# First two blocks of a fused chunk-attention and FFN kernel: only the first third of the FFN columns in halves of 128 tokens

## The chip, the cores and the metric

The kernel runs on one core of one Trainium2 chip. The metric is the device time of one execution in microseconds (us); smaller is better. Eight runs of the kernel before stand behind its median. The profile is of one further execution, and its own times are used wherever a sum is made.

## The reference

Attention over chunks, followed by a gated feed-forward network (FFN). The inputs are float32, with batch 4, 8 heads, 768 tokens and a head dimension of 64; the FFN has 3072 tokens, a model width of 512 and 1536 FFN columns.

```python
k_min, k_max = k_chunks.min(3), k_chunks.max(3)        # chunks of 32 tokens
ub = sum(maximum(q * k_min, q * k_max))                # upper bound by query and chunk
top_chunks = argsort(where(causal, ub, -1e9))[..., -6:]
scores = where(sel & causal_by_token, q @ k.T / sqrt(D), -1e9)
x = (softmax(scores) @ v)                              # heads side by side: 3072 x 512
xn = x / sqrt(mean(x * x) + 1e-6) * rms_g
g = xn @ w_gate
out = (g * sigmoid(g) * (xn @ w_val)) @ w_out
```

## The kernel before

The work is cut into 12 blocks of 256 tokens, in the order of `ORDER` (line 398): the first block of each batch element, then later ones. A block belongs to one batch element `b` and a third `m` of its tokens. For each block, and for each of two groups of four heads, `job` (line 626) does the attention. DVE transposes K and Q (line 642), the copies `kb` and `qb` in bf16 are made on ACT or POOL (lines 649, 650), DVE reduces K to the minimum and maximum of each chunk (line 657), and DVE or POOL writes them into block-diagonal matrices BD (line 669). `pick` (line 531) multiplies these with Q on TensorE (line 562, the upper bounds), finds the six best chunks on DVE and turns the result into masks. TensorE makes scores and adds the masks (lines 720, 731), ACT takes the exponential into `pt` (line 770), POOL cuts the triangle off (line 740), TensorE multiplies with the values (line 796), and DVE divides by the row sum into `xnat` (lines 811, 815).

`norm` (line 822) follows. ACT squares and sums `xnat` (line 831), POOL makes the reciprocal root (lines 837, 839), DVE or ACT scales to `xs` (lines 847, 849), TensorE transposes (line 859), and DVE or ACT multiplies with `rms_g` into `xsT` (lines 872, 868).

`ffn` (line 879) then goes over the FFN columns. There are 12 tiles of 128 columns; the three thirds of the gate, value and output weights (`wg`, `wv`, `wo`) are loaded by nine transfers on POOL's queue (lines 516 and 521). For each step, TensorE makes one PSUM bank of gate products and one of value products (line 897), with 512 columns each: two column tiles for the 256 tokens of a block, or four for 128 tokens. ACT takes the tanh (`th`, line 904), DVE makes `tg` from it (line 908), and the product with the values, `hh`, is made in one of two ways: DVE reads the values from PSUM (line 912, the steps in `DIRECT`, line 407), or ACT copies them to `vs` (line 916) and POOL multiplies (line 919). TensorE multiplies `hh` with `wo` (line 929), and ACT or DVE takes the result to `osb` (lines 943, 945), which SP stores (line 950).

Blocks 0 and 1 are in `SPLIT` (line 404): `HALVES` (line 409) cuts them into two halves of 128 tokens, and both `norm` and `ffn` are called for each half. So a half goes through all three thirds of the columns by itself, in three steps of four column tiles. Each half takes one of the four `xsT` buffers.

Nothing of the order is left to the hardware or to a compiler. `plan.op` records each operation with its engine, an expected occupation and latency, and a priority; `Plan.run` (line 160) walks through a modelled time and gives each engine, at each point, the operation of the lowest priority number that could start. What comes out is a fixed order for each engine, and each engine works through its own from front to back. The priorities come from due times: `due_attn(i) = PACE * i - LEAD` and `due_ffn(i) = PACE * i` (lines 412 to 416), with offsets by step. Operations recorded with `flex` may go to one of two engines, and the walk chooses. `PATIENT` (line 120) lets an engine look a little ahead for an urgent operation. Where TensorE would be idle in the modelled time before 60 us, the walk puts in matmuls of constants (line 995), called filler here; they are executed.

SP issues the loads of K, Q and V of the blocks in order, and stores between them. `HELD` (line 475) makes a load wait for a weight transfer: for block 2 the first K load waits for the first gate third and the first V load for the first value third, and for block 3 both wait for the first third of `wo`. SP issues in order, so everything behind such a load waits too. There are two buffers for raw K, three for raw Q, two for raw V, four PSUM banks F (gate, value, output, value products and transposes) and two double banks S (scores and upper bounds).

The softmax here doesn't subtract the row's maximum and nothing guards it: scores larger than these inputs give would overflow.

## Time and profile before

| | |
|---|---|
| median of 8 runs | 305.92 us (305.17 to 306.32) |
| the profiled execution | 305.85 us |
| its span, first to last instruction | 304.1 us, granted TensorE clock 1.000 |
| gate and value matmuls (line 897) | 192 + 192 of 128 columns, 480 + 480 of 256 |
| output matmuls (line 929) | 288 of 512 columns |
| filler (line 995) | 86 of 128 columns, 36 of 512 in the program, 29 of these in the records |
| nine weight transfers (POOL's queue) | issued from 10.8 to 21.3 us |
| `hh` on POOL (line 919), on DVE (line 912) | 51 of 1.164 us, 21 of 0.687 us |

A row of the page's groups gives the line, engine, operation, what is written and read, shapes, count, busy time, mean duration, and the idle time before with what ended it. A row of a timeline gives the start, the duration, the engine and line, and in brackets the idle time before and its releaser. A row of windows gives a stretch and then, for each engine, the time in which it was busy. Matmuls overlap, so the start of one group to the start of the next is the better measure of its cost than the duration given. A few matmul records are missing from the trace.

### The profile page before, as it was taken

Reading aid. Unit: us, or ns where it says so; the run is one execution under the profiler, and the core shown is the slowest. Engines: PE = TensorE matmul, PEld = TensorE weight load, DVE = VectorE, ACT = ScalarE, POOL = GpSimd, SP = SyncE. Lnnn points to the kernel's source line nnn. Section 1 sums busy time; section 2 is a strip of 40 time slices with the busy share of each in tenths; the row PEclk is TensorE's granted clock in tenths of the full one; section 3 lists DMA queues with packets and bytes.
Section 4 is the critical chain, followed back from the end, with each engine's and each line's share of the span. In section 5 each row is a group of like instructions: output and inputs, shape, how many; then the busy total and the mean of one; then the engine's idle time right before and its main releaser. Section 6 shows DMA issues by size and latency. Waiting matters only on the chain.

```text
span 304.1 us, 11660 instructions
## 1 busy us (share of the span) xinstructions
PE 289.5 (95%) x4830; PEld 223.4 (73%) x4858; DVE 218.7 (72%) x565; ACT 217.4 (71%) x382; POOL 147.2 (48%) x267
## 2 busy tenths in 40 slices
PE   8777999999999999999999999999999999999994
PEld 8445897767958876885887787688588688588671
DVE  6997797886799999999999697286457254356250
ACT  3574975779987996997797856698767588476240
POOL 4694568758572784687456413235213143123130
PEclk9999999999999999999999999999999999999999
DMA  7999995775766556565850200100010010010101
GB/s 195 221 197 263 196 205 119 162 200 121 192 152 160 126 120 160 129 147 120 195 128 0 72 2 4 69 5 3 2 71 2 2 71 3 34 39 1 69 2 69
DMA packets 74837, 30.65 MB, mean 101 GB/s; under 512 B 65568, under 2 KB 70176, under 8 KB 74784
## 3 DMA queue, kind: packets, MB, share of 16 engines
q1 hardware_dynamic: 69184, 24.66, 33.4%
q0 software_dynamic: 4752, 4.72, 9.3%
q8 instruction: 38, 0.62, 0.8%
q10 hardware_dynamic: 848, 0.53, 0.6%
q14 instruction: 15, 0.12, 0.2%
HBM read 28.31 MB, written 6.29 MB: 114 GB/s over the span
## 4 chain that ended last, share of the span: by engine, by line
PE 76%; DVE 5%; ACT 2%; issue 1%
PE F L897 34%; PE F L929 20%; PE S L720 7%; PE F L796 6%; PE S L562 5%; PE S L731 2%; PE F L859 1%; DVE kx L657 1%; DVE tg L908 1%; ACT pt L770 1%; DVE xnat L815 1%; ACT junk L831 0%; DVE qT L642 0%; ACT xs L849 0%; DVE m L597 0%
## 5 line engine op out<-in xcount | busy, mean ns | idle before, releaser
L919 POOL TENSOR_TENSOR hh<-tg,vs 128x512 bf16<-128x512 bf16 x51 | 59.3, 1164 | 83.0 <-ACT vs L916 62.3
L770 ACT ACTIVATE pt<-S 128x1024 bf16<-128x1024 f32 (+3 forms) x104 | 86.2, 860 | 18.3 <-PE S L731 17.6
L897 PE MATMUL F<-xsT,wg 128*128 128x256 bf16 (+1 forms) x672 | 74.9, 257 | 2.3 <-DMA wg<-in_moe_w_gate_dram 1.6
L897 PE MATMUL F<-xsT,wv 128*128 128x256 bf16 (+1 forms) x672 | 74.9, 257 | 2.1 <-DMA wv<-in_moe_w_val_dram 1.3
L908 DVE SCALAR_TENSOR_TENSOR tg<-th,F 128x512 bf16<-128x512 bf16 x72 | 48.8, 680 | 36.7 <-ACT th L904 36.0
L929 PE MATMUL F<-wo,hh 128*128 128x512 bf16 x267 | 64.4, 379 | 1.7 <-issue 1.0
L897 PEld LDWEIGHTS <-wg 128*128 128x128 bf16 x672 | 56.6, 98 | 10.3 <-DMA wg<-in_moe_w_gate_dram 2.1
L897 PEld LDWEIGHTS <-wv 128*128 128x128 bf16 x672 | 56.8, 98 | 9.4 <-DMA wv<-in_moe_w_val_dram 1.5
L904 ACT ACTIVATE th<-F 128x512 bf16<-128x512 f32 x72 | 43.3, 602 | 17.1 <-PE F L897 15.7
L929 PEld LDWEIGHTS <-hh 128*128 128x128 bf16 x288 | 26.5, 98 | 28.5
L740 POOL TENSOR_SCALAR_AFFINE_SELECT pt<-pt 128x512 bf16<-128x512 bf16 x48 | 30.5, 645 | 18.1 <-ACT pt L770 17.4
L916 ACT ACTIVATE vs<-F 128x512 bf16<-128x512 f32 x51 | 30.7, 601 | 6.3 <-PE F L897 5.4
L720 PE MATMUL S<-qb,kb 32*128 32x256 bf16 (+1 forms) x800 | 32.6, 253 | 1.4 <-ACT qb L649 1.2
L657 DVE TENSOR_REDUCE kx<-kT 128x16 f32<-128x512 f32 x48 | 30.3, 663 | 0.0
L796 PE MATMUL F<-VX,pt 128*128 128x65 bf16 x672 | 26.7, 194 | 0.9 <-ACT vs L916 0.4
L796 PEld LDWEIGHTS <-pt 128*128 128x128 bf16 x672 | 24.2, 98 | 3.7 <-issue 1.1
L831 ACT ACTIVATE junk<-xnat 128x512 bf16<-128x512 bf16 x24 | 15.1, 627 | 14.2 <-DVE xnat L815 12.4
L720 PEld LDWEIGHTS <-kb 32*128 32x128 bf16 x800 | 13.6, 92 | 14.5 <-issue 13.7
L945 DVE TENSOR_SCALAR osb<-F 128x512 f32<-128x512 f32 x14 | 9.5, 687 | 17.6 <-PE F L929 17.6
L815 DVE TENSOR_TENSOR xnat<-F,rden 128x256 bf16<-128x256 f32 x48 | 19.8, 421 | 1.1
L731 PE MATMUL S<-mtd,chunkrow 32*128 32x128 bf16 (+2 forms) x384 | 20.3, 203 | 0.0
L731 PE MATMUL S<-mto,chunkrow 32*128 32x128 bf16 (+2 forms) x384 | 19.8, 202 | 0.0
(61 smaller groups left out, 357.0 us busy)
## 6 DMA issues: line engine op xcount, KB each, us to landing
vraw<-in_v_dram SPq DMA_DIRECT2D x24, 256.0 KB, 4.1
out_dram<-osb SPq DMA_DIRECT2D x24, 256.0 KB, 2.2
kraw<-in_k_dram SPq DMA_DIRECT2D x72, 64.0 KB, 3.0
qraw<-in_q_dram SPq DMA_DIRECT2D x72, 64.0 KB, 2.3
wg<-in_moe_w_gate_dram POOLq DMA_DIRECT2D x3, 512.0 KB, 14.0
wv<-in_moe_w_val_dram POOLq DMA_DIRECT2D x3, 512.0 KB, 17.0
wo<-in_moe_w_out_dram POOLq DMA_DIRECT2D x3, 512.0 KB, 24.6
kraw<-in_k_dram SPq DMA_DIRECT2D x10, 128.0 KB, 4.8
```

The costliest lines, as they stand in the source:

```text
L657: plan.op(f"ext{n}{J}", "DVE", 0.585, 0.67, lambda n=n, op=op: VE.tensor_reduce(out=at(kx)[:, n], in_=at(kT).rearrange("p h (c t) -> p h c ...
L720: TE.matmul(s[a // 2][:, a % 2, c0:c0 + q1 - q0], kbt[r, t, ks], qbt[r, t, q0:q1], start=(t == 0), stop=(t == 1 and not mask), skip_group_ ...
L731: TE.matmul(o, chunkrow[r, BLK * kg + P * e:BLK * kg + P * (e + 1)], mv, start=False, stop=(d == 1), skip_group_check=True)
L740: GE.affine_select(out=d, in_=d, compare_op=ALU.is_ge, fill=0.0, base=0, pattern=[[0, 4], [1, P]], channel_multiplier=-1)
L770: lambda pt=pt, hs=hs, c0=c0, c1=c1, x=sc[hp]: SE.activation(out=at(pt)[:, hs, c0:c1], in_=at(x)[:, :, c0:c1], func=ACT.Exp, scale=SCALE), ...
L796: TE.matmul(o[:, a, :], p_[:, a, off:off + P], vt[:, e, a, :], start=(kb_ == 0 and a == 0), stop=(kb_ == nkb - 1 and a == 3), skip_group_c ...
L897: TE.matmul(at(p_)[:, n * W:(n + 1) * W], w[:, g, ht * P:(ht + 1) * P], at(xT)[:, g, 0:W], start=(g == 0), stop=(g == NP - 1), skip_group_ ...
L904: plan.op(f"tanh{U}.{hp}", "ACT", 0.48, 0.6, lambda th=th, gp=gp: SE.activation(out=at(th), in_=at(gp), func=ACT.Tanh, scale=0.5), pri - 0 ...
L908: VE.scalar_tensor_tensor(out=at(tg), in0=at(th), scalar=1.0, in1=at(gp), op0=ALU.add, op1=ALU.mult), pri - 40, reads=[th, gp], writes=[tg ...
L916: plan.op(f"vcopy{U}.{hp}", "ACT", 0.48, 0.6, lambda vs=vs, vp=vp: SE.activation(out=at(vs), in_=at(vp), func=ACT.Copy), pri + 0.1, reads= ...
L919: plan.op(f"hh{U}.{hp}", "POOL", 1.11, 1.16, lambda tg=tg, vs=vs, hh=hh: GE.tensor_tensor(out=at(hh), in0=at(tg), in1=at(vs), op=ALU.mult) ...
L929: TE.matmul(at(op)[:], at(("hh", *U, ht // K))[:, o:o + P], wo[:, ht, :], start=(ht == 0), stop=(ht == NHT - 1))
```

## The change

For blocks 0 and 1, `norm` still goes by halves, but both halves write into one `xsT` buffer of 256 tokens, each into its own columns. `ffn` is called once for a block. It makes a list of pieces: for a block in `SPLIT`, the first third of the columns (four column tiles) for the first 128 tokens, the same for the second 128 tokens, and then the remaining eight tiles for all 256 tokens, two tiles at a time. The other blocks have six pieces of two tiles, as before. The output product picks its rows of `hh` from either kind of piece; its last step now has two column tiles in all blocks.

Beside this some settings change. Block 2's K and V loads both wait for the second gate third, and block 3's V load for the second `wo` third. `DIRECT` holds blocks 8 to 11 in place of 5 to 11, so nine `hh` products go from DVE to ACT and POOL. `PACE` and `LEAD` are 22.5 and 70 in place of 23.5 and 73, `PATIENT` is empty, and the priorities of tanh, of the direct `hh`, of the output product, of the output copy and of the first halves' `norm` differ. In the built program the gate and value matmuls are 64 + 64 of 128 columns and 544 + 544 of 256, and there are 38 wide fillers.

```diff
 
 
     SHARES = ("scale", "relu", "bd0", "bd1", "dk", "mk")
-    PATIENT = {"DVE": 0.3}
+    PATIENT = {}
     RESERVED = ("hh",)
     HOP = {"PE": 0.055, "ACT": 0.04, "DVE": 0.04, "POOL": 0.075, "SP": 0.06}
 
...
     ORDER = [(0, 0), (1, 0), (2, 0), (3, 0), (0, 1), (1, 1), (0, 2), (2, 1), (1, 2),
              (3, 1), (2, 2), (3, 2)]
     assert sorted(ORDER) == [(b, m) for b in range(B) for m in range(NBLK)]
-    PACE, LEAD = 23.5, 73
+    PACE, LEAD = 22.5, 70
     MARGIN = 2.0
     FIRST = 8
     SPLIT = {0, 1}
     APART = {0, 1}
     PACKED = {0, 1, 2}
-    DIRECT = {(i, hp) for i in range(len(ORDER)) for hp in range(KH) if i >= 5 and hp % 2}
+    DIRECT = {(i, hp) for i in range(len(ORDER)) for hp in range(KH) if i >= 8 and hp % 2}
 
     def HALVES(i):
         return ((0,), (1,)) if i in SPLIT else ((0, 1),)
...
     ones = [("ones", i) for i in range(len(store["VX"]))]
 
 
-    HELD = {2: (("wg", 0), ("wv", 0)), 3: (("wo", 0), ("wo", 0))}
+    HELD = {2: (("wg", 1), ("wg", 1)), 3: (("wo", 0), ("wo", 1))}
 
     def load_qk(i, nm, src):
         b, m = ORDER[i]
...
         blk = b * NBLK + m
         n = len(toks)
         U = (i, toks)
-        xT, tp = ("xsT", *U), ("tp", *U)
+        xT, tp = ("xsT", i), ("tp", *U)
+        cols = slice(toks[0] * P, (toks[-1] + 1) * P)
         for s in toks:
             xn, tt = ("xnat", b, m, s), 2 * blk + s
             plan.op(f"square{i}{s}", "ACT", 0.61, 0.82, lambda xn=xn, tt=tt: SE.activation(
...
 
         def rows():
             for g in range(NP):
-                SE.activation(out=at(xT)[:, g, 0:n * P], in_=tview()[:, g], func=ACT.Copy,
+                SE.activation(out=at(xT)[:, g, cols], in_=tview()[:, g], func=ACT.Copy,
                               scale=rmsg[:, g:g + 1])
 
         flex(f"xsT{U}", {
             "DVE": (0.07 + 0.53 * n, 0.15 + 0.53 * n, lambda: VE.tensor_tensor(
-                out=at(xT)[:, :, 0:n * P], in0=tview(),
+                out=at(xT)[:, :, cols], in0=tview(),
                 in1=rmsg[:].unsqueeze(2).to_broadcast([P, NP, n * P]), op=ALU.mult)),
-            "ACT": (0.6 + 0.43 * n, 0.72 + 0.43 * n, rows)}, base, reads=[tp, "rmsg"], writes=[xT],
-            takes=[(xT, "xsT")])
-
-
-    def ffn(i, toks):
+            "ACT": (0.6 + 0.43 * n, 0.72 + 0.43 * n, rows)}, base, reads=[tp, "rmsg"] + (
+                [xT] if toks[0] else []), writes=[xT + (s,) for s in toks],
+            takes=[] if toks[0] else [(xT, "xsT")])
+
+
+    def ffn(i):
         b, m = ORDER[i]
-        U = (i, toks)
-        W = P * len(toks)
-        K = 512 // W
-        KH = NHT // K
-        base = due_ffn(i) + toks[0]
-        xT = ("xsT", *U)
-        for hp in range(KH):
-            third = 3 * hp // KH
+        xT = ("xsT", i)
+        whole = (0, 1)
+        cut = NHT // 3 if i in SPLIT else 0
+        pieces = [((s,), h) for s in whole for h in range(0, cut, 4)] + [
+            (whole, h) for h in range(cut, NHT, 2)]
+        for toks, h0 in pieces:
+            W = P * len(toks)
+            K = 512 // W
+            U = (i, toks)
+            hp = h0
+            base = due_ffn(i) + toks[0]
+            third = 3 * h0 // NHT
+            x0 = P * toks[0]
             gp, vp = ("gp", *U, hp), ("vp", *U, hp)
             th, vs, tg, hh = ("th", *U, hp), ("vs", *U, hp), ("tg", *U, hp), ("hh", *U, hp)
-            pri = base + hp * 6 // KH
+            pri = base + h0 // 2
             for nm, p_, w in (("wg", gp, wg), ("wv", vp, wv)):
-                def gate(p_=p_, w=w, hp=hp):
+                def gate(p_=p_, w=w, h0=h0, K=K, W=W, x0=x0):
                     for n in range(K):
-                        ht = K * hp + n
+                        ht = h0 + n
                         for g in range(NP):
                             TE.matmul(at(p_)[:, n * W:(n + 1) * W],
-                                      w[:, g, ht * P:(ht + 1) * P], at(xT)[:, g, 0:W],
+                                      w[:, g, ht * P:(ht + 1) * P], at(xT)[:, g, x0:x0 + W],
                                       start=(g == 0), stop=(g == NP - 1), skip_group_check=True)
 
                 o = plan.op(f"{nm}{U}.{hp}", "PE", 0.873, 1.035, gate, pri,
-                            reads=[xT, (nm, third)], writes=[p_], takes=[(p_, "F")])
+                            reads=[xT, (nm, third)] + [xT + (s,) for s in toks], writes=[p_], takes=[(p_, "F")])
                 o.mode = "full"
             plan.op(f"tanh{U}.{hp}", "ACT", 0.48, 0.6, lambda th=th, gp=gp: SE.activation(
-                out=at(th), in_=at(gp), func=ACT.Tanh, scale=0.5), pri - 0, reads=[gp], writes=[th],
+                out=at(th), in_=at(gp), func=ACT.Tanh, scale=0.5), pri - 20, reads=[gp], writes=[th],
                 takes=[(th, "th")])
             plan.op(f"tg{U}.{hp}", "DVE", 0.6, 0.69, lambda th=th, gp=gp, tg=tg:
                     VE.scalar_tensor_tensor(
                         out=at(tg), in0=at(th), scalar=1.0, in1=at(gp), op0=ALU.add,
                         op1=ALU.mult), pri - 40, reads=[th, gp], writes=[tg], takes=[(tg, "tg")])
-            if (i, hp) in DIRECT:
+            if (i, h0 // 2) in DIRECT:
                 plan.op(f"hh{U}.{hp}", "DVE", 0.6, 0.69, lambda tg=tg, vp=vp, hh=hh: VE.tensor_tensor(
-                    out=at(hh), in0=at(tg), in1=at(vp), op=ALU.mult), pri - 40, reads=[tg, vp],
+                    out=at(hh), in0=at(tg), in1=at(vp), op=ALU.mult), pri - 30, reads=[tg, vp],
                     writes=[hh], takes=[(hh, "hh")])
                 continue
             plan.op(f"vcopy{U}.{hp}", "ACT", 0.48, 0.6, lambda vs=vs, vp=vp: SE.activation(
...
             plan.op(f"hh{U}.{hp}", "POOL", 1.11, 1.16, lambda tg=tg, vs=vs, hh=hh: GE.tensor_tensor(
                 out=at(hh), in0=at(tg), in1=at(vs), op=ALU.mult), pri - 40, reads=[tg, vs],
                 writes=[hh], takes=[(hh, "hh")])
-        for k_, s in enumerate(toks):
+        for s in whole:
             op, ob = ("op", i, s), ("osb", i, s)
-            last = NHT - K
-
-            def project(h0, h1, k_=k_, op=op):
+            last = NHT - 2
+
+            def part(ht, s=s):
+                if ht < cut:
+                    return ("hh", i, (s,), ht // 4 * 4), ht % 4 * P
+                return ("hh", i, whole, ht // 2 * 2), ht % 2 * BLK + s * P
+
+            def project(h0, h1, s=s, op=op, part=part):
                 for ht in range(h0, h1):
-                    o = (ht % K) * W + k_ * P
-                    TE.matmul(at(op)[:], at(("hh", *U, ht // K))[:, o:o + P], wo[:, ht, :],
+                    key, o = part(ht)
+                    TE.matmul(at(op)[:], at(key)[:, o:o + P], wo[:, ht, :],
                               start=(ht == 0), stop=(ht == NHT - 1))
 
-            pri = base + 8 + s
+            base = due_ffn(i)
+            hhs = sorted({part(ht)[0] for ht in range(last)}, key=str)
+            pri = base + 6 + s
             o = plan.op(f"project{i}.{s}", "PE", 0.216 * last, 0.216 * last + 0.17,
                         lambda project=project: project(0, last), pri,
-                        reads=[("hh", *U, x) for x in range(KH - 1)] + [("wo", x) for x in range(3)],
+                        reads=hhs + [("wo", x) for x in range(3)],
                         writes=[op], takes=[(op, "F")])
             o.mode = "full"
-            o = plan.op(f"project{i}.{s}+", "PE", 0.216 * K, 0.216 * K + 0.17,
+            o = plan.op(f"project{i}.{s}+", "PE", 0.216 * 2, 0.216 * 2 + 0.17,
                         lambda project=project: project(last, NHT), pri - 20,
-                        reads=[("hh", *U, KH - 1), op], writes=[op])
+                        reads=[part(NHT - 1)[0], op], writes=[op])
             o.mode = "full"
             flex(f"out{i}.{s}", {
                 "ACT": (0.48, 0.6, lambda op=op, ob=ob: SE.activation(
                     out=at(ob), in_=at(op), func=ACT.Copy, scale=0.5)),
                 "DVE": (0.6, 0.69, lambda op=op, ob=ob: VE.tensor_scalar(
                     out=at(ob), in0=at(op), scalar1=0.5, scalar2=None, op0=ALU.mult))},
-                pri - 0, reads=[op], writes=[ob], takes=[(ob, "osb")])
+                pri - 20, reads=[op], writes=[ob], takes=[(ob, "osb")])
             r0 = b * S + BLK * m + P * s
             o = plan.op(f"store{i}.{s}", "SP", 0.46, 0.46, lambda ob=ob, r0=r0: SY.dma_start(
                 out=out[r0:r0 + P, :], in_=at(ob)), pri, reads=[ob])
...
             for j in jobs:
                 next(j, None)
         for toks in HALVES(i):
-            norm(i, toks, due_attn(i) + (7 if toks[-1] else -12))
+            norm(i, toks, due_attn(i) + (7 if toks[-1] else -3))
         if i == 0:
             for n in range(3):
                 load_w(n, -290 if n == 0 else -36 + n)
...
                 if o.dma and o.eng == "POOL":
                     o.after.append(first_dk[0])
     for i in range(len(ORDER)):
-        for toks in HALVES(i):
-            ffn(i, toks)
+        ffn(i)
 
     def keep_busy(n, slot, wide):
         for _ in range(n):
```

## Prediction

> **What bounds the kernel now.** I read the busy table and the slices of the page first. TensorE (PE) leads, and its slices say when it is not full:
>
> ```profile
> PE 289.5 (95%) x4830; PEld 223.4 (73%) x4858; DVE 218.7 (72%) x565; ACT 217.4 (71%) x382; POOL 147.2 (48%) x267
> PE   8777999999999999999999999999999999999994
> DMA  7999995775766556565850200100010010010101
> ```
>
> Only the first four slices (7.6 us each), about 30 us, and the last lack 9s. Even those 7s flatter it: line 995 is filler (matmuls of a constant that keep the array busy), so I read the windows of that line, where PE is busy 6.55 us of the first 8 us, 4.29, 2.28, 1.20 and 0.38 us of the next 8 us stretches, then nothing. Useful work is thin until about 37 us and dense after. The windows of all engines, then PE's own waits between 60 and 200 us:
>
> ```profile
> 32.00:40.00 8.00, 7.83 (x163) 7.21 (x162) 6.54 (x15) 7.36 (x17) 5.75 (x8) 1.00 1.21 196
> 40.00:48.00 8.00, 7.37 (x144) 7.02 (x142) 7.57 (x13) 5.53 (x11) 5.59 (x14) 1.00 1.02 180
> 144.00:168.00 24.00, 23.79 (x445) 19.17 (x447) 22.66 (x59) 19.19 (x34) 13.16 (x25) 1.00 0.47 109
> ...
> PE F L897 <- DVE xnat L815: 0.4, 1, 0.4
> PE F L796 <- ACT vs L916: 0.4, 1, 0.4
> PE F L796 <- ACT osb L943: 0.2, 1, 0.2
> ```
>
> (columns: PE, weight loads, DVE, ACT, POOL, clock, DMA share). From 60 to 200 us PE waits 1.0 us for other engines. So the end is set by when PE becomes dense, plus its work from there on. What holds the front is in PE's timeline:
>
> ```profile
> 19.14 1.07 PE L897 MATMUL F<-xsT,wg 128*128 128x128 bf16 x16
> 23.00 1.07 PE L897 MATMUL F<-xsT,wv 128*128 128x128 bf16 x16 [1.33 <-DMA wv<-in_moe_w_val_dram]
> 27.82 1.07 PE L897 MATMUL F<-xsT,wg 128*128 128x128 bf16 x16 [1.63 <-DMA wg<-in_moe_w_gate_dram]
> 29.89 1.05 PE L897 MATMUL F<-xsT,wg 128*128 128x128 bf16 x16 [0.18 <-DVE xsT L872]
> 47.66 0.43 PE L562 MATMUL S<-qT,BD 64*64 64x32 f32 x16
> ```
>
> The first gate third is used as it lands (19.1), the first value third ends a wait at 23.0, and the gate's second third a wait of 1.63 us at 27.8. Behind that last one stands the transpose of block 0's second half. 47.66 is the start of block 2's upper bounds (line 562): my landmark.
>
> **What the Trainium skill says.** "TensorE: Matmul & The Clock Gate", section "Wait — 56ns, not 53.3ns?", gives a warm matmul N / 2.4 GHz plus 2.5 ns: 55.6 ns for 128 columns, so 109.2 ns for 256. The trace agrees: eleven value and gate groups at the end take 9.61 us for 88 matmuls, 109.2 ns, and groups of sixteen 128-column matmuls start 0.89 us apart (40.10, 40.99, 41.88), 55.6 ns. The same page, section "Architectural detail", says that ACT and DVE take instructions strictly in order; so a DVE transpose that waits for a transfer holds all DVE work behind it. "DMA: Bandwidth & Descriptors", section "Queues, rings and completion order", says each DMA engine takes turns between the queues that have work, packet by packet. The trace agrees: the weight loads on POOL's queue land 3.3 to 3.5 us apart once the other loads have thinned out (31.5, 34.9, 38.2, 41.7) and 3.9 and 4.7 us apart (19.1, 23.0, 27.7) while SP's loads of block 2 share.
>
> **The change part by part.** For PE order, I compared the instruction order of both built programs. At the landmark both have done the same: FFN worth 144 matmuls of 256 columns, 160 score, 48 value and 16 transpose matmuls. Their last 49 groups are the same, and both switch 130 times between kinds of matmul that load the array in different shapes. So only the landmark's time, the matmul widths and later waits count.
>
> Widths: 256 matmuls of 128 columns become 128 of 256; 16 groups of sixteen at 0.89 us become 16 groups of eight at 0.874: 0.26 us off, 0.1 of it after the landmark. Filler: 38 wide ones instead of 36, 2 x 0.22 = +0.44 us, but all before 28 us, where the path below goes past them.
>
> Front, PE's path. The wait of 1.63 us for the second gate third goes: its first reader now stands after the first third of both halves. Next late is the value third. Block 2's K, Q and V now wait for the second gate third instead of the first, so nothing of them shares, and it should land 3.4 us after 19.1, at 22.5. Behind it now stands the value product of block 0's second half, once ahead of it. From there: value group 0.9, that product 0.35 (23.75), reciprocal and scaling 0.6, square 0.82, POOL's root 0.85, scaling on ACT 0.73, transpose 0.4, DVE's xsT 0.69, and hops: in the trace of before these steps take 5.6 us with DVE's other work between, 4.4 without; I take 5 and have the second half's first gate group at 28.7 (29.89 before). From there to the landmark PE has ten groups of 256 columns (8.74), six of 128 (5.34), three value products (1.1), scores 0.53, two transposes 0.66: 16.4 us, so 45.1, and 46.0 with the 0.8 to 0.9 us of small bank waits that the same stretch has now.
>
> Front, DVE's path. This is the added wait. SP waits for the second gate third with block 2's K, Q and V queued behind. Now:
>
> ```profile
> 19.16 2.62 SPq L422 DMA_DIRECT2D kraw<-in_k_dram  x4
> DMA to landing us min/median/max: 6.8/6.8/6.8
> 33.48 1.11 DVE L642 STREAM_TRANSPOSE kT<-kraw 128x512 f32<-128x512 f32 x1
> ```
>
> (the second line is of the last of these four issues, at about 21.3). K lands at 28.1, 8.9 us after the first issue, and is not used until 33.48; that idle cover of 5.4 us is what the new wait eats. The second gate third should land at 19.1 + 2 x 3.4 = 25.9, so K at 34.8 with the same sharing, or about 33.9 if it is quicker now that block 1's V (landing to 24.8) is out of the way. From K's first transpose DVE has, in its new order up to the last block-diagonal write: four transposes 3.9, six tg 3.7, four reductions 2.4, two xsT 1.2, two xnat 0.7, small ones 0.5: 12.4 us, plus 0.25 for a hop to the matmul. Landmark 46.5 to 47.5 without idle. It lies behind PE's 46.0, so it decides: I take 46.9, 0.76 us earlier than now. Both ends stay for the range: 46.0, and 49.2 if DVE also idles the 1.7 us that it idles in this stretch now.
>
> Later. Block 3's V waits for the second wo third (44.5 now) and isn't issued before 52.1; K waits as now: nothing. POOL issues the wo loads some casts and selects later, but they queue behind a load that lands at 38.2: nothing unless they come after that. Nine products move from DVE to ACT and POOL in blocks 5 to 7: 9 x 0.687 = 6.2 us off DVE, 9 x 0.601 = 5.4 on ACT, 9 x 1.164 = 10.5 on POOL. The 144 to 168 row shows room on POOL (13.2 of 24) and ACT (19.2), while DVE is at 94%; about half of it falls there. The other constants (pace, lead, priorities) only reorder. All this can touch only waits: 1.0 us to win between 60 and 200, an open amount to lose. I take 0.2 off, and keep 0.9 off and 1 on as ends.
>
> Sum: 0.76 + 0.1 + 0.2 = 1.06 us off. The profiled execution took 305.85 with a span of 304.1 (1.75 around it), so span 303.0 and 304.8; the median of the runs, 305.92, lies 0.07 above, so 304.9.
>
> **The rivals.** (1) *K takes the place of the weight wait, evenly.* Landmark at 47.5, what is left is the 0.1: 305.8. For it: K's landing falls just where DVE wants it. Against: 33.9 to 34.8 leaves DVE packed, which it is already in 40 to 48 (7.57 of 8). (2) *K late, slower.* K lands at 34.8, at DVE's head; the six tg behind it free PSUM buffers, PE runs dry, and DVE idles its 1.7 us besides: landmark 49.2, plus 1.5, less 0.1: 307.3. It decides as soon as K's transpose starts after about 34.0 with that idle, 35.7 without. For it: the 1.33 and 1.63 us waits show weights landing later than the order allows for. Against: DVE's idle now stems partly from the wait that goes. (3) *Both paths open.* DVE is not in the way (46.0, 1.66 off), and the relieved DVE ends most later waits (0.9), and 0.1: 303.3. Against: K would have to land by 33.3. (4) *The change doesn't do what it says:* excluded, the built program has 128 gate and value matmuls of 128 columns where it had 384.
>
> **How the numbers follow.** The likeliest, 304.9: 0.47. Rival 3: 0.10. Rival 1: 0.18. Rival 2: 0.25. 0.2%, 0.6 us, is about what a measurement of this kernel can tell from no change. Faster is the first two, 0.57; same is rival 1, 0.18; slower is rival 2, 0.25. The range, 303.2 to 307.2, takes in rival 3 and the lower half of rival 2's spread; the likeliest alone spans 304.2 to 305.3.
>
> **What would show it.** Right: no wait for the second gate third on PE; the first value group near 22.5; block 2's K issued near 26 and DVE's transpose of it waiting on its transfer; block 2's upper bounds near 46.9; PE's waits after 60 us near 1 us. Wrong: that landmark after 47.7 (rival 2), or waits of PE on POOL's hh or on ACT past 60 us, which I have not priced beyond 1 us.

## The result, and the profile after

The changed kernel takes 303.83 us (median of 12 runs, 302.84 to 305.24) against 305.74 us for the kernel before on the same chip (32 runs, 305.03 to 306.32): a ratio of 0.9941 with a 95% interval of 0.9929 to 0.9952, so 1.5 to 2.2 us faster. Its profiled execution took 304.21 us with a span of 302.5; before, 305.85 and 304.1. The traces therefore have 1.64 us to explain, and a single execution of the changed kernel can lie a microsecond either way.

The page of the changed kernel, the same rows as before:

```profile
PE 290.6 (96%) x4703; PEld 222.4 (74%) x4732; DVE 205.8 (68%) x540; ACT 220.1 (73%) x396; POOL 166.7 (55%) x293
PE   8898899998999999999999999999999999999994
DMA  7999994875766557476740100100010110110101
```

VectorE has lost 12.9 us of work and GpSimd gained 19.5. The nine moved products account for 6.2 and 11.0 of that; the rest are other operations that the new plan put on other engines. The first four slices of TensorE are fuller (8898 for 8777). The windows of all engines and TensorE's waits between 60 and 200 us, again the same rows:

```profile
32.00:40.00 8.00, 7.44 (x88) 6.51 (x87) 7.96 (x15) 7.12 (x16) 5.73 (x10) 1.00 1.20 215
40.00:48.00 8.00, 7.89 (x152) 7.16 (x150) 6.20 (x13) 6.30 (x12) 6.19 (x9) 1.00 0.86 164
144.00:168.00 24.00, 23.73 (x420) 18.66 (x422) 19.78 (x52) 18.80 (x31) 18.41 (x33) 1.00 0.36 87
```

```profile
PE F L904 <- DVE xnat L815: 0.6, 1, 0.6
PE F L941 <- issue: 0.3, 2, 0.2
PE F L796 <- DVE tg L915: 0.2, 1, 0.2
PE F L941 <- POOL kb L650: 0.2, 1, 0.2
```

VectorE is at 7.96 of 8 us between 32 and 40 us, but no longer between 40 and 48 (6.20; 7.57 before), nor in 144 to 168 (19.78; 22.66 before). The four waits of the second list sum to 1.3 us. The 1.0 us that the prediction read before had counted named releasers only; one line stood beside them:

```profile
PE F L929 <- issue: 0.8, 5, 0.2
```

Counted alike, the named waits are 1.0 us in both kernels, and the gaps without a releaser fell from 0.8 to 0.3: nothing was won there in named waits, and nothing lost. Now TensorE's timeline in the front, where the forecast put the gain:

```profile
21.58 1.07 PE L904 MATMUL F<-xsT,wv 128*128 128x128 bf16 x16 [0.20 <-DMA wv<-in_moe_w_val_dram]
27.95 1.07 PE L904 MATMUL F<-xsT,wg 128*128 128x128 bf16 x16
30.82 0.22 PE L904 MATMUL F<-xsT,wv 128*128 128x128 bf16 x1 [0.96 <-issue]
32.15 1.04 PE L904 MATMUL F<-xsT,wg 128*128 128x256 bf16 x8
37.03 2.80 PE L904 MATMUL F<-xsT,wg 128*128 128x256 bf16 x32 [0.52 <-DVE xsT L873]
46.42 0.43 PE L562 MATMUL S<-qT,BD 64*64 64x32 f32 x16
```

The wait for the first value third is 0.20 us instead of 1.33. The wait of 1.63 us for the gate's second third is gone: its first reader is the group at 32.15, and by then it has long been there. The second half's first gate group stands at 27.95 instead of 29.89. New is a gap of 0.96 us ahead of 30.82. The profile gives it no releaser ("issue"); what is next in TensorE's order is a value product whose triangle GpSimd finishes at 30.44, 0.38 us ahead, so I take it for that wait; the trace doesn't show it. Block 2's upper bounds start at 46.42, 1.24 us earlier than before. The chain that ended last shows how the two paths to that landmark are tied (columns: start, length, what):

```profile
13.63 10.49 DMA wg<-in_moe_w_gate_dram
...
25.50 7.38 DMA kraw<-in_k_dram
32.88 0.02 issue
32.90 1.13 DVE kT L642
...
37.78 1.16 POOL hh L926
...
41.91 4.59 PE F L904 x64
46.49 1.07 PE S L562 x64
```

The gate's second third lands at 24.1, SyncE then issues block 2's K, its last piece lands at 32.88, and VectorE's transpose starts 0.02 us later: the cover that K had before is used up to the last. (That cover was 6.2 us, not the 5.4 of the prediction: the last of K's four issues stands at 20.47, not 21.3, so K had landed at 27.3.) But the chain doesn't stay on VectorE. It goes over GpSimd and ScalarE to TensorE's own groups from 41.91 on, which run without a gap into the bounds.

### The profile page after: what moved, and what is told of

Its sections match the earlier page's. It is cut to its first block, busy times and chain, and to the rows that moved or that the text cites. A ratio compares the mean times of both kernels' runs of the same rounds, so it can differ in the third digit from the quotient of the medians.

```text
span 302.5 us, 11439 instructions
## 1 busy us (share of the span) xinstructions
PE 290.6 (96%) x4703; PEld 222.4 (74%) x4732; DVE 205.8 (68%) x540; ACT 220.1 (73%) x396; POOL 166.7 (55%) x293
## 4 chain that ended last, share of the span: by engine, by line
PE 76%; DMA 9%; POOL 5%; DVE 4%; ACT 2%; issue 2%; SPq 1%; ACTq 0%; DVEq 0%; POOLq 0%
PE F L904 35%; PE F L941 17%; PE F L796 7%; PE S L720 7%; PE S L562 6%; DMA wg<-in_moe_w_gate_dram 3%; DMA kraw<-in_k_dram 3%; DMA qraw<-in_q_dram 3%; PE S L731 3%; POOL hh L926 2%; PE F L860 1%; SPq L422 1%; DVE kT L642 1%; DVE qT L642 1%; POOL pt L740 1%
## 5 line engine op out<-in xcount | busy, mean ns | idle before, releaser
L926 POOL TENSOR_TENSOR hh<-tg,vs 128x512 bf16<-128x512 bf16 x60 | 70.1, 1173 | 67.3 <-ACT vs L923 46.0
L770 ACT ACTIVATE pt<-S 128x1024 bf16<-128x1024 f32 (+3 forms) x104 | 87.2, 862 | 20.6 <-PE S L731 20.2
L941 PE MATMUL F<-wo,hh 128*128 128x512 bf16 x264 | 65.2, 379 | 1.6 <-issue 0.3
L904 PEld LDWEIGHTS <-wv 128*128 128x128 bf16 x608 | 55.5, 98 | 9.0 <-issue 1.3
L904 PEld LDWEIGHTS <-wg 128*128 128x128 bf16 x608 | 55.5, 98 | 8.6 <-issue 0.6
L941 PEld LDWEIGHTS <-hh 128*128 128x128 bf16 x288 | 26.6, 98 | 27.6
L923 ACT ACTIVATE vs<-F 128x512 bf16<-128x512 f32 x60 | 35.9, 612 | 9.9 <-PE F L904 8.7
L796 PEld LDWEIGHTS <-pt 128*128 128x128 bf16 x672 | 24.1, 98 | 4.4 <-issue 2.4
L959 DVE TENSOR_SCALAR osb<-F 128x512 f32<-128x512 f32 x12 | 8.2, 688 | 24.0 <-PE F L941 24.0
```

What stands on the lines that cost most here:

```text
L770: lambda pt=pt, hs=hs, c0=c0, c1=c1, x=sc[hp]: SE.activation(out=at(pt)[:, hs, c0:c1], in_=at(x)[:, :, c0:c1], func=ACT.Exp, scale=SCALE), ...
L796: TE.matmul(o[:, a, :], p_[:, a, off:off + P], vt[:, e, a, :], start=(kb_ == 0 and a == 0), stop=(kb_ == nkb - 1 and a == 3), skip_group_c ...
L904: TE.matmul(at(p_)[:, n * W:(n + 1) * W], w[:, g, ht * P:(ht + 1) * P], at(xT)[:, g, x0:x0 + W], start=(g == 0), stop=(g == NP - 1), skip_ ...
L923: plan.op(f"vcopy{U}.{hp}", "ACT", 0.48, 0.6, lambda vs=vs, vp=vp: SE.activation(out=at(vs), in_=at(vp), func=ACT.Copy), pri + 0.1, reads= ...
L926: plan.op(f"hh{U}.{hp}", "POOL", 1.11, 1.16, lambda tg=tg, vs=vs, hh=hh: GE.tensor_tensor(out=at(hh), in0=at(tg), in1=at(vs), op=ALU.mult) ...
L941: TE.matmul(at(op)[:], at(key)[:, o:o + P], wo[:, ht, :], start=(ht == 0), stop=(ht == NHT - 1))
```

## A ruler for the plans

Most variants below are planned anew, so their TensorE orders differ and a start time alone compares different amounts of work. I therefore subtract from the start of a group of upper bounds the TensorE work that the program puts ahead of it, each kind priced at the spacing of its dense groups (0.1092 us for a gate or value matmul of 256 columns, 0.0558 for 128, 0.216 for a projection, 0.056 for a transpose; filler at nothing). What is left is called *lost*. It says nothing absolute, but plans can be compared by it. "Front" is lost up to block 2's upper bounds, "rest" is what is added from there to the last block's upper bounds (at 220 to 225 us; the plans of e5 and e6 have them already at 208 and 206, so their rest leaves out what is lost behind that).

| kernel | median us | ratio, 95% interval | front | rest |
|---|---|---|---|---|
| before | 305.7 | 1 | 26.11 | 18.40 |
| changed | 303.83 | 0.9941 (0.9929, 0.9952) | 25.06 | 18.12 |
| structure only (e1) | 306.08 | 1.0013 (1.0006, 1.0020) | 24.61 | 20.41 |
| settings only (e2) | 306.50 | 1.0025 (1.0012, 1.0038) | 27.18 | 19.55 |
| changed, block 2's loads early (e3) | 304.06 | 0.9952 (0.9933, 0.9971) | 24.51 | 18.12 |
| changed, planner's settings back (e5) | 304.32 | 0.9955 (0.9942, 0.9967) | 24.37 | 17.99 |
| changed, 256 columns as twice 128 (e4) | 304.30 | 0.9952 (0.9934, 0.9969) | 24.94 | 18.06 |
| changed, priorities back (e6) | 305.29 | 0.9988 (0.9980, 0.9996) | 24.07 | 18.48 |
| changed, DIRECT back (e7) | 306.06 | 1.0015 (1.0006, 1.0025) | 24.28 | 19.26 |
| changed, no wide filler (e8) | 305.39 | 1.0000 (0.9983, 1.0017) | 24.99 | 18.54 |
| before, block 2's loads late (e9) | 305.17 | 0.9981 (0.9974, 0.9987) | 25.21 | 18.48 |
| two thirds in halves (e10) | 306.60 | 1.0037 (1.0022, 1.0051) | 24.15 | 20.31 |
| no halves (e11) | 305.58 | 0.9998 (0.9988, 1.0009) | 24.97 | 19.54 |
| DIRECT from the tenth block (e12) | 304.11 | 0.9954 (0.9937, 0.9972) | 24.74 | 18.12 |

Front and rest are of one profiled execution each. The changed kernel, e3 and e12 have the same order up to about 235 us: their fronts differ by up to 0.55 us (landings vary), their rests not at all (18.12 three times). The kernel before and e9 have one order too, with 18.40 and 18.48, and e8 has the changed kernel's without the wide filler, with 18.54. So a difference of 0.5 in front is noise, and of the rest only what goes well beyond 0.4 can be put down to the order. The row of e2 is of its slowest execution (308.10 us, 1.6 over its median), so its two numbers are too high by an unknown part.

The ruler also splits the 1.64 us between the two profiled executions: 1.05 in front, 0.28 in the rest, and 0.31 for the widths, which it prices as work.

## The experiments

**Structure and settings apart.** The change is a piece structure and a set of constants; each was put alone on the other's kernel.

e1, on the changed kernel:

```diff
-    PATIENT = {}
+    PATIENT = {"DVE": 0.3}
-    PACE, LEAD = 22.5, 70
+    PACE, LEAD = 23.5, 73
-    DIRECT = {(i, hp) for i in range(len(ORDER)) for hp in range(KH) if i >= 8 and hp % 2}
+    DIRECT = {(i, hp) for i in range(len(ORDER)) for hp in range(KH) if i >= 5 and hp % 2}
-    HELD = {2: (("wg", 1), ("wg", 1)), 3: (("wo", 0), ("wo", 1))}
+    HELD = {2: (("wg", 0), ("wv", 0)), 3: (("wo", 0), ("wo", 0))}
...
-            pri = base + 6 + s
+            pri = base + 8 + s
```

and with them the other priorities of the change: tanh 0 for -20, VectorE's product -40 for -30, the output copies 0 for -20, the first half's norm -12 for -3.

> The changed FFN pieces alone, with all settings of before (pace, lead, patience, direct products, holds and priorities), planned anew. Theory (the front decides, by the order of the thirds and by the held loads together): the second gate third is no longer waited for, but block 2's loads share with the weights again, so the first value third lands near 23.0 and not 21.5; the upper bounds of block 2 come at about 47, and the time is about 0.7 us below before (305.0). Rival (the settings make the gain later in the kernel): no different from before, 305.7.

Measured: 306.08 us, slower than both sides expected. Its upper bounds of blocks 2 and 3:

```profile
47.72 0.43 PE L562 MATMUL S<-qT,BD 64*64 64x32 f32 x16
...
60.19 0.38 PE L1008 MATMUL F<-chunkrow,ident 128*128 128x512 bf16 x1 [0.50 <-DVE xnat L815]
60.62 2.32 PE L941 MATMUL F<-wo,hh 128*128 128x512 bf16 x10
62.87 0.43 PE L562 MATMUL S<-qT,BD 64*64 64x32 f32 x16
```

47.72 looks like no gain, but this order has 16 gate and value matmuls more behind it by then (1.75 us): front 24.61, a gain of 1.5. The theory had expected the first value third near 23.0, since block 2's loads are no longer held; it landed at 21.4. The gain is given back twice. Block 3's bounds come at 62.87, with a filler and projections put right ahead of them, against 59.20 in the changed kernel: between the two landmarks e1 loses 2.03 us by the ruler and the changed kernel 0.95. About 1.2 us more go by up to the last block. So the pieces win the front under the old settings too, and the old settings' plan loses it again.

e2, on the kernel before: the same constants the other way round.

> The settings of after alone, on the half-by-half FFN of before, planned anew. Theory: with block 2's loads held, the second gate third lands near 24 and its wait of 1.6 us on TensorE mostly goes without the new pieces; but the halves need all thirds early. About 0.5 to 1 us below before (305.0). Rival (the settings make all of the gain, by the products moved off DVE): 1.6 to 1.9 us below, 303.9, with block 2's upper bounds no earlier than 47.7 and the time won after 60 us.

Measured: 306.50 us, where both sides had expected a gain. The settings alone gain nothing; they lose 0.4 to 1.2 us. Where isn't shown: front and rest (27.18 and 19.55) are both worse, but in that slowest execution.

**The later release of block 2's loads.** e3 keeps every instruction of the changed kernel in its order, and only releases block 2's K, Q and V as before:

```diff
+    FENCE = {("load k2", ("wg", 1)): ("wg", 0), ("load q2", ("wg", 1)): ("wg", 0), ("load v2", ("wg", 1)): ("wv", 0)}
...
-        fences = [p for key in behind for p in plan.wrote[key]]
+        fences = [p for key in behind for p in plan.wrote[FENCE.get((name[:7], key), key)]]
```

> After with its order of instructions kept on every engine; only the wait of block 2's K and Q loads (first gate third) and V load (first value third) is that of before. Theory (holding the loads pays, since the value third and what hangs on it come earlier): the first value group starts near 23.0 in place of 21.6, block 2's upper bounds near 47.6 in place of 46.4, and the time is about 1.0 to 1.2 us above after (304.9). Rival (the added wait costs, K at the head of DVE): K lands near 28, DVE does not wait for it, and the time is 0.3 to 0.8 us below after (303.3).

Measured: 304.06 us, the same as the changed kernel. In its timeline (lines are one further down here and in e9):

```profile
22.03 0.95 PE L905 MATMUL F<-xsT,wv 128*128 128x128 bf16 x14 [0.76 <-DMA wv<-in_moe_w_val_dram]
45.87 0.43 PE L563 MATMUL S<-qT,BD 64*64 64x32 f32 x16
```

K is issued at 19.03 instead of 24.18, and the gate's second third lands at 26.1 instead of 24.1; its first reader stands at 31.8, so nobody notices. The first value third lands at 22.0 instead of 21.5, which is within what it varies by. Both theories expected the release to matter, and both missed. Four of the 17 executions, the slowest (305.42 to 306.69), had a granted clock of 0.991 to 0.994; the other 13 have their median at 303.86. None of the changed kernel's 12 was below 0.996. Whether the release has to do with that isn't shown.

e9 makes the opposite step on the kernel before, order kept: block 2's K, Q and V are held until the gate's second third has landed.

```diff
+    FENCE = {("load k2", ("wg", 0)): ("wg", 1), ("load q2", ("wg", 0)): ("wg", 1), ("load v2", ("wv", 0)): ("wg", 1)}
...
-        fences = [p for key in behind for p in plan.wrote[key]]
+        fences = [p for key in behind for p in plan.wrote[FENCE.get((name[:7], key), key)]]
```

> The kernel before, order of all instructions kept, with block 2's K, Q and V loads held until the second gate third has landed (before: behind the first gate and the first value third). Theory (halves need the second gate third before the second half has had any work; the hold is not where the gain is, as the run with early loads in the changed kernel says): the weights land up to 2.5 us sooner and TensorE's two early waits for weights (1.33 and 1.63 us) shrink, but K comes later by as much or more, block 2's upper bounds start at 47.2 to 48.5, and the time is 305.3 to 306.3. Rival (the hold alone brings the gain): landmark 46.3 to 46.8, time 304.2 to 304.9.

Measured: 305.17 us, 0.57 us faster (0.4 to 0.8), between the two ranges; the start of the bounds, 46.76, is the rival's. Its timeline:

```profile
21.91 1.07 PE L898 MATMUL F<-xsT,wv 128*128 128x128 bf16 x16 [0.51 <-DMA wv<-in_moe_w_val_dram]
25.32 1.06 PE L898 MATMUL F<-xsT,wg 128*128 128x128 bf16 x16
46.76 0.43 PE L563 MATMUL S<-qT,BD 64*64 64x32 f32 x16
...
23.87 1.74 SPq L423 DMA_DIRECT2D kraw<-in_k_dram  x4
32.62 1.12 DVE L643 STREAM_TRANSPOSE kT<-kraw 128x512 f32<-128x512 f32 x1
```

The same two groups that waited 1.33 and 1.63 us before now wait 0.51 and nothing. And K, issued 4.7 us later, is transposed at 32.62, 0.86 us *earlier* than before. What the queues moved between 18 and 30 us tells why (packets, MB, share), the kernel before:

```profile
q0 software_dynamic: 1609, 1.60, 78.8%
q1 hardware_dynamic: 1378, 1.23, 39.0%
```

and e9:

```profile
q0 software_dynamic: 2184, 2.17, 109.1%
q1 hardware_dynamic: 265, 0.45, 11.7%
```

About the same in all (2.83 and 2.62 MB), but the weights' queue has 2.17 MB of it instead of 1.60. That fits what the Trainium skill says in "DMA: Bandwidth & Descriptors", section "Queues, rings and completion order": engines take turns between queues with work. K needed by 33 us was being paid for with weights needed by 26.

This holds for the gate's second third, not for the first value third, whose wait the prediction also put down to block 2's loads. Between 18 and 22 us SyncE's queue moved 0.13 MB in the kernel before, nothing in e1 and 0.01 MB in e3, although all three had issued block 2's K by 19.2. The 0.13 MB were block 1's V, the one load under way there besides (532 packets of about 250 bytes; K's have 2048): its last piece landed at 24.2 in the kernel before, at 16.4 in e1 and 21.0 in e3, and the value third at 23.0, 21.4 and 22.0. In e5, with the hold, V landed at 22.8 and the value third at 22.5. So the 1.33 us wait goes with a landing that varies from execution to execution. The gate's second third landed at 23.4 to 25.2 in the eleven profiles with the hold, and at 27.8, 25.2 and 26.1 in the three without (before, e1, e3).

So e3 and e9 together: the 1.63 us wait can be taken away by using the second third later (the pieces) *or* by landing it sooner (the hold). The changed kernel does both; the second of them adds nothing that a measurement shows.

**The narrow matmuls.** e4 keeps the changed kernel's order and splits each matmul of 256 columns of the first two blocks into two of 128.

```diff
-                        for g in range(NP):
-                            TE.matmul(at(p_)[:, n * W:(n + 1) * W],
-                                      w[:, g, ht * P:(ht + 1) * P], at(xT)[:, g, x0:x0 + W],
+                        for c in range(0, W, P) if i in SPLIT else (0,):
+                            w1 = P if i in SPLIT else W
+                            for g in range(NP):
+                                TE.matmul(at(p_)[:, n * W + c:n * W + c + w1],
+                                          w[:, g, ht * P:(ht + 1) * P], at(xT)[:, g, x0 + c:x0 + c + w1],
```

> After with its order kept; in blocks 0 and 1 each gate or value matmul of 256 columns is made as two of 128 on the same PSUM bank, so the widths alone are undone. Theory: 128 more matmul pairs cost 16 groups by 0.016 us, 0.26 us, at most hidden in part (304.0). Rival (the second weight load of each pair is not hidden): 128 loads by up to 0.098 us more, up to 12 us, or visibly more than 0.5 us.

Measured: 304.30 us (0.9952, 0.9934 to 0.9969), 0.3 us over the changed kernel by the ratios. This is the size forecast, 0.26, but the two intervals overlap, so the sign isn't shown. By the ruler nothing else changed (24.94 and 18.06).

**Which settings keep the gain.** Three groups of constants were put back one at a time, each planned anew.

e5:

```diff
-    PATIENT = {}
+    PATIENT = {"DVE": 0.3}
-    PACE, LEAD = 22.5, 70
+    PACE, LEAD = 23.5, 73
```

> The changed kernel with only the planner's two settings put back (PATIENT for VectorE 0.3, PACE/LEAD 23.5/73), planned anew. Its first 34 us of TensorE work come out in the same order as in the run with all settings put back (306.08 us). Theory (the pieces win about 1.1 to 1.5 us ahead of block 2's upper bounds, and the planner's settings are what keeps it between 48 and 63 us): the front is won again, but block 3's upper bounds lie late by about 1 us, and the time is 305.5 to 306.2. Rival (the priorities of tanh, product, projection and copies keep it, not the planner's): 303.6 to 304.4.

Measured: 304.32 us. This is in the rival's range: the planner's settings hardly matter (the intervals of e5 and of the changed kernel overlap).

e6:

```diff
-            pri = base + 6 + s
+            pri = base + 8 + s
...
-                pri - 20, reads=[op], writes=[ob], takes=[(ob, "osb")])
+                pri - 0, reads=[op], writes=[ob], takes=[(ob, "osb")])
...
-            norm(i, toks, due_attn(i) + (7 if toks[-1] else -3))
+            norm(i, toks, due_attn(i) + (7 if toks[-1] else -12))
```

and likewise tanh 0 and VectorE's product -40.

> The changed kernel with only the priorities put back (tanh 0 instead of -20, VectorE's product -40 instead of -30, projection base 8 instead of 6, output copies 0 instead of -20, late filler -12 instead of -3), planned anew. The first 40 us are almost in the changed kernel's order, so block 2's upper bounds start at 46.4 +- 0.7 under both theories. Theory (the planner's settings keep the gain): 303.6 to 304.4. Rival (the priorities keep it): the lead is lost after 48 us and the time is 305.3 to 306.2.

Measured: 305.29 us, 1.5 over the changed kernel: the lower edge of the rival's range. But the front is not lost (24.07), and the rest, up to 206 us, is only 0.36 worse, in the execution that was profiled. That execution took 304.57 and was the fastest of 21; where the other 0.7 us lie isn't shown.

e7:

```diff
-    DIRECT = {(i, hp) for i in range(len(ORDER)) for hp in range(KH) if i >= 8 and hp % 2}
+    DIRECT = {(i, hp) for i in range(len(ORDER)) for hp in range(KH) if i >= 5 and hp % 2}
```

> The changed kernel with only DIRECT put back (9 more products on VectorE straight from PSUM in the sixth to eighth block, their 9 ScalarE copies and 9 GpSimd products gone), planned anew. Order is the same up to about 150 us, so the first landmark is at 46.4 +- 0.5. Theory (what is kept is decided before 65 us): 303.6 to 304.4. Rival (part of the gain is in the middle of the span, where VectorE has 9 x 0.6 = 5.4 us less to do in the changed kernel): 304.6 to 305.4, with new PE waits on VectorE after 120 us.

Measured: 306.06 us, more than either expected. This loss has a place. TensorE's waits between 60 and 270 us begin, in e7, with

```profile
PE S L562 <- ACT pt L770: 1.1, 1, 1.1
```

and the timeline there reads

```profile
154.21 0.62 PE L860 MATMUL F<-ident,xs 128*128 128x128 bf16 x8
155.89 0.67 PE L562 MATMUL S<-qT,BD 64*64 64x128 f32 x16 [1.07 <-ACT pt L770]
```

The upper bounds need a bank that ScalarE's exponentials of a score tile leave at 155.75. The changed kernel has the same neighbours, but its plan puts a value group between the transposes and the bounds:

```profile
155.88 0.61 PE L860 MATMUL F<-ident,xs 128*128 128x128 bf16 x8
156.32 1.04 PE L904 MATMUL F<-xsT,wv 128*128 128x256 bf16 x8
157.29 0.67 PE L562 MATMUL S<-qT,BD 64*64 64x128 f32 x16
```

So DIRECT acted here not by VectorE's load but by what the planner had left to put into that gap. This wait of 1.07 us is nearly all that the rest loses (1.14), and half of the 2.2 by the medians; the profiled execution also ended with a slower last store (0.6 us longer to land), and the remainder isn't located.

e12 goes one block further in the other direction:

```diff
-    DIRECT = {(i, hp) for i in range(len(ORDER)) for hp in range(KH) if i >= 8 and hp % 2}
+    DIRECT = {(i, hp) for i in range(len(ORDER)) for hp in range(KH) if i >= 9 and hp % 2}
```

> The changed kernel with DIRECT from the tenth block on instead of the ninth: 3 more products go to GpSimd with 3 more ScalarE copies. Same order up to about 235 us. Theory (the cost of putting DIRECT back was one wait of TensorE at 155 us for ScalarE's exponentials, a matter of that place, not of VectorE's load): nothing is gained or lost at this end, 303.6 to 304.3. Rival (fewer products on VectorE are better everywhere): 303.0 to 303.5.

Measured: 304.11 us, the same as the changed kernel. Three fewer products on VectorE made nothing better here.

**The filler.** e8 takes the wide filler matmuls out of the changed kernel, order kept.

```diff
-        for _ in range(n):
+        for _ in range(0 if wide else n):
```

> The changed kernel, order of all instructions kept, with the filler matmuls of 512 columns taken out that the plan puts into TensorE's gaps (their results are never read). It leaves out no part of the computation. Theory (as predicted: filler stands in gaps only and costs nothing): 303.8 +- 0.3, with the gaps now empty. Rival (some filler lies on the path, 0.22 us each, since the gaps on the chip aren't where the plan has them): faster by up to a third of their sum, 301.5 to 303.2. A third way: without them the clock falls, and the time is over 304.5.

Measured: 305.39 us (1.0000, 0.9983 to 1.0017): the gain of the whole change is gone, as the third way had it. The page's row of the granted clock:

```profile
PEclk9968999999999999999999999999999999999998
```

and the windows of all engines in the front (the clock is the third number from the end):

```profile
12.00:16.00 4.00, 2.23 (x84) 1.77 (x85) 3.45 (x20) 1.75 (x5) 4.00 (x7) 0.76 1.27 207
16.00:20.00 4.00, 3.01 (x72) 2.29 (x68) 3.93 (x7) 3.91 (x13) 3.92 (x8) 0.50 1.24 206
28.00:32.00 4.00, 3.84 (x70) 3.78 (x68) 0.70 (x4) 2.53 (x6) 0.99 (x2) 0.60 1.16 278
```

With the filler the clock is 1.00 in each of these stretches. Without it it falls to 0.50, and the group that takes 1.05 us in the changed kernel takes

```profile
19.66 1.67 PE L904 MATMUL F<-xsT,wg 128*128 128x128 bf16 x16
```

The Trainium skill says so ("TensorE: Matmul & The Clock Gate", section "What's actually happening": "the default state is throttled, and activity releases the throttle"), at half the clock. In the profiled execution the slow groups still fitted into slack (bounds at 46.4 as in the changed kernel, 304.55 us in all); it was the second fastest of 13. Over these 13 the time rises as the mean granted clock falls: from 304.49 us at 0.983 to 307.14 at 0.965, where the changed kernel's executions all had 0.996 or more. So the loss goes with the clock; no trace of a slower execution shows the groups that pay for it.

**How much in halves.** e10 and e11 change one size, planned anew with the changed kernel's settings.

```diff
-        cut = NHT // 3 if i in SPLIT else 0
+        cut = 2 * NHT // 3 if i in SPLIT else 0
```

in e10, and `cut = 0` in e11.

> The changed kernel with two thirds of the columns of the first two blocks in halves instead of one, planned anew with the changed kernel's settings. Theory (the gain in front is that the second half's work on the first third stands ahead of the second gate third): with two thirds in halves the first half's work needs the second gate third earlier, time lost on TensorE up to block 2's upper bounds (their start less the TensorE work ahead of them) is 25.3 to 26.5 us, against 25.06 in the changed kernel and 26.1 before, and the time is 304.6 to 305.8. Rival (the extent doesn't matter, only the plan and its settings do): lost 24.0 to 25.1, time 303.6 to 304.4.

Measured: 306.60 us. The front (24.15) is no worse than with one third, which is the rival's number and not the theory's; the time is neither's. The rest is 20.31, 2.2 more than in the changed kernel. Its one long wait after 48 us:

```profile
PE F L904 <- ACT vs L923: 1.3, 1, 1.3
```

> The changed kernel with no columns in halves at all: every group of the first two blocks waits for all 256 tokens; planned anew. Theory (the first third in halves fills TensorE from 19 to 28 us, until the second half's tokens are there): about 3 to 5 us of that stage are empty, some of it refilled with scores and values; lost up to block 2's upper bounds 27 to 30, time 306 to 309. Rival (the second half's tokens can be had by 22 us, and the first weights bind, not the tokens): 303.5 to 304.5.

Measured: 305.58 us, between the two ranges. My theory, 3 to 5 us of emptiness, was wrong. The first gate group waits for all 256 tokens until 26.75, but up to that time the changed kernel has only two groups of sixteen ready (1.8 us); e11 puts filler there, has the second half's tokens in use 1.2 us sooner than the changed kernel (27.95), and reaches the bounds with the same lost time (24.97). It then loses 19.54 in the rest.

So the front was gained with two thirds, one third and nothing in halves (24.15, 25.06, 24.97, against 26.11 before). In none of the three does TensorE wait for the gate's second third, which lands at 23.7 to 24.8 behind the held loads; in e10 its first reader even stands at 24.96, ahead of the second half's first group, as in the kernel before. So the front didn't need the extent of one third. That extent was best here by the rest alone, that is by the plan that came out of it.

## Why the prediction was right, and where it was off

303.83 us lies in the range of the prediction, but below the 304.2 to 305.3 that its likeliest case spans: the gain was 1.9 us where 1.06 was forecast. Between the profiled executions the landmark gained 1.24 us (0.76 forecast), the widths behind it 0.1 (0.1) and the rest 0.28 (0.2). So it was the landmark that was mis-sized.

*The bound and the landmark: right.* TensorE stays dense from the front on, and 1.24 of the 1.64 us between the profiled executions stand at the landmark. The upper bounds of block 3 come 1.34 us sooner (59.20 for 60.54), the last transposes 1.63 (273.29 for 274.92).

*The wait for the gate's second third goes: right, and shown twice*, by the changed kernel's timeline and by e9, which removes the same wait without the pieces.

*The pace of the weights, the term most off.* I took 3.4 us from one weight load's landing to the next, read from a stretch at 31 to 42 us in which other loads still shared (0.08 MB in each 2 us), and called it unshared. They land at 19.0, 21.5, 24.1 and 26.6: 2.5 to 2.6 us apart. From this one number follow the value third at 21.5 (I had 22.5), the gate's second third at 24.1 (25.9), the second half's first group at 27.95 (28.7) and K at 32.88 (33.9 to 34.8). The 8.9 us from K's first issue to its landing came near the 8.7 measured by luck: before they were 8.2, misread as told above. And that block 2's loads had delayed the value third was a wrong reading: block 1's V had (e1, e3).

*TensorE's path: 46.0 forecast, 46.42 measured.* It began 0.75 us earlier than I had it and lost more: 1.7 us of waits from the second half's first group to the landmark (0.96, 0.52 and 0.2) where I carried over 0.8 to 0.9. The largest, 0.96, is the gap ahead of 30.82. The start of this very stretch gained time, so what had been hidden behind the start became visible.

*VectorE's path decides: wrong.* From K's transpose to the last block-diagonal write it took 12.8 us (32.90 to 45.67), forecast 12.4. With K at 32.88 that is ready at 45.7, 45.9 with the hop, and TensorE reaches the bounds at 46.42, without a gap ahead. TensorE's path decided, by half a microsecond; the two I had in the opposite order. The later release itself costs nothing that a measurement shows (e3 without it: the same time): K lands 6.3 us later than in e3 (26.58), and still at VectorE's turn.

*Widths, 0.26: in line with e4*, not resolved from nothing.

*Filler, no cost: incomplete.* No run prices the two that were added. I named the path that goes past the filler. It also holds the clock (e8), which the profile before, with 1.00 in every stretch, could not show.

*Later, 0.2 off: the size was right (0.28 by the ruler), the reason wasn't.* I expected the relief of VectorE to end waits. The named waits after 60 us stayed at 1.0 us; and 0.28 is no more than the rest can differ by with one order (e8). What the settings do is choose another order; put back one group at a time, they cost 0.5 (planner, not resolved from nothing), 1.5 (priorities) and 2.2 us (DIRECT), together with the hold 2.2 (e1). They don't add up, and where one of them was followed (e7) it acted by the order and not by an engine's load. I had called this term an open amount; it is as large as the whole gain.

*The rivals.* K evenly late (bounds at 47.5) and K late (49.2) fell with K's landing at 32.88. The third, both paths open with K by 33.3 at the latest, had its condition met; it was not reached because TensorE's path lost 0.4 and the later waits gave nothing. 303.83 lies between it (303.3) and the forecast (304.9), nearer to the rival, which I had given 0.10. (The first rival's sum is off by 0.1: 0.16 and 0.1 off 305.92 make 305.7, not 305.8.)

*What stays open.* Neither the pieces alone (e1) nor the settings alone (e2) are faster; together they are, with or without the hold (e3) and the planner's settings (e5). Why these orders lose so little behind the front was followed only in part. In e6, e7 and e10 the median lies 0.4 to 0.7 us above the profiled execution, and nothing profiled says where. The give-back of e1, e10 and e11 in the rest was followed only at single waits of 0.5 to 1.3 us. No variant had a lower median than the changed kernel.

## What to carry to other kernels

Where several queues load at once, a transfer that has slack can take its bandwidth from one that has none (once K was held in e9, the weights' queue moved 2.17 MB where it had moved 1.60): look for the landing that is idle longest before its use (here K, 6.2 us) and hold it behind the one that is waited for; holding it, or using the late one later, are two ways to the same gain and didn't add here. When a planner draws the order, an edit's effect is its own stage *and* a new order for everything behind it; here the second cost up to 2.3 us, more than the stage had gained, so compare an edit with the order held as well as planned anew. And before taking filler away as useless, look at what the clock does without it.

## What the hardware showed that I had not expected

Finer windows of e8 show when the clock changed: it was 1.00 up to 14.1 us, 0.50 to 20.9, 1.00 to 27.8, 0.50 to 31.2, and 1.00 from there. These times lie about 3.4 or 6.8 us apart. In the 3.4 us ahead of each fall TensorE was busy 2.11 us (10.7 to 14.1) and 1.90 us (24.4 to 27.8), with no idle time longer than 1.1 us in either; in two such stretches after which the clock stayed at 1.00 it was busy 2.44 us (7.3 to 10.7) and 2.81 us (20.9 to 24.4). So being busy for over half of a stretch was not enough to hold it. The Trainium skill ("TensorE: Matmul & The Clock Gate", section "What's actually happening") puts the fall "after ≥1 idle window (~3.4µs)". The length fits; but here such a stretch counted as idle although TensorE worked in it for some 2 us. That is one trace, and where the line lies between 2.11 and 2.44 us isn't shown.

With no other load beside them, three weight loads landed 2.5 to 2.6 us apart (19.0, 21.5, 24.1 and 26.6 in the changed kernel, where SyncE's queue moved nothing from 18 to 26 us). In the kernel before, the same loads were 3.9 us apart with block 1's V beside them (19.1 to 23.0) and 4.8 with block 2's loads (23.0 to 27.8).

And three executions of one order, to within three products at its end, had their front at 24.5 to 25.1 us and everything behind it equal to 0.01 us: what varied between them lay in the first 46 us. Three are few; the twelve of the changed kernel spread over 2.4 us.
